# Attention events of the last three passes of a unit, placed without the clamp

## The chip, the cores and the metric

One NeuronCore of a Trainium2 chip runs the kernel. The metric is device time in microseconds (us): the median of three runs. Five engines work side by side, each through its own instructions in order: PE (TensorE, matrix products, with PEld for its weight loads), DVE (VectorE), ACT (ScalarE), POOL (GpSimd) and SP (SyncE, which here issues transfers only). PE writes its results to eight PSUM banks, from which ACT and DVE read them.

## What is computed

```python
def _attn_ref(q, k, v):                       # 8 batches, 12 heads, 448 tokens, 64 wide
    scale = 1.0 / np.sqrt(q.shape[-1])
    scores = scale * np.matmul(q, k.transpose(0, 1, 3, 2))
    attn = np.maximum(scores, 0.0) ** 2 / S
    return np.matmul(attn, v)
...
x = attn_out.transpose(0, 2, 1, 3).reshape(B * S, H * D)   # 3584 x 768
gate = np.maximum(x @ w_gate, 0.0)            # 768 x 1536
val = x @ w_val
out = gate * val @ w_out                      # 1536 x 768
```

Attention with squared ReLU in place of softmax, and behind it a gated feed-forward layer over all 3584 tokens. Inputs and output are float32; the products run in bf16.

## The kernel before

The kernel overlaps two kinds of work on PE: the attention of one batch, and the gate and value products of the batch before.

**Gate/value units.** `gv_units(b)` gives twelve units for batch b, each for 128 of the 1536 hidden columns. A unit (`gv_unit`, L302) is a list of twelve steps, here called passes 0 to 11; a pass is four matmuls of 64x64 weights by 448 tokens (`mm4`, recorded on L72, `ps<-x,gv`). All twelve passes add into one pair of banks, 6 and 7 or 4 and 5 in turn (`acc`). In the last pass ACT writes the ReLU of the gate half to `g_sb` (L320) and DVE multiplies it with the value half into `hT` (L321). Then the pair is free for the unit after next.

**Attention events.** A batch has 21 score tiles and 3 values events.
- A score tile (`scores_event`, L657) is four matmuls (`ps<-kqT`) into a pair of banks; ACT writes the ReLU of both banks to `r_sb` (L232) and DVE squares that into `attn` (L233).
- A values event (`values_event`, L660) is 28 matmuls (`ps<-attn,vn`) into a pair of banks; ACT reads the first bank (L266) and DVE the second (L267), and DVE copies halves across partitions (L261). For the last two batches both engines read parts of both banks (L276, L277).
- All of them take turns on two pairs, banks 0 and 1 and banks 2 and 3 (`sc_later`). So an event can start once the pair of the event before last has been read.

In this text 7.12 is score tile 12 of batch 7, and "values 5.1" is the second values event of batch 5. A place 6:8 is unit 6 of the list, ahead of pass 8.

**Where events go.** The main loop (L745) runs over b = 1 to 6. In each turn the units of batch b - 1 are the frame (ten of them at b = 1, since two were begun before; twelve otherwise). For b = 1 to 4 the events of batch b are spread over them, and for b = 5 and 6 a stream of all that is left of batches 5, 6 and 7. `stream` lists the events in order, and `paced` (L724) gives each a place: it lays out the passes from `first` to `behind` in a row, computes a gap in passes per event (3.8 to 4.4 at b = 1, 2, 5 and 6, and 6.2 at b = 3 and 4, with shorter gaps around values events), and sets each event ahead of the pass at which it falls due. The place is then clamped: where the due pass is 9, 10 or 11 of its unit, the event goes ahead of pass 8 (`len(units[u]) - 4`). Some other events are placed by hand and not by `paced`: the third values event of batches 1 to 4 and of 7 (`last`, 8 or 5), the transposes, the regroup copies with DMA transposes (`turned`), weight sums and loads. `spread` (L686) sorts all events by place and issues them between the passes; every instruction is pinned to the program's order on its engine.

The six turns are six stretches of the run: b = 1 from 36 to 65 us, b = 2 to 102 us, then the output products of the first two batches (`out_pair`), b = 3 from 126 to 161 us, b = 4 to 196 us, output products again, b = 5 from 220 to 261 us, b = 6 to 302 us. After that come output products and the gate/value products of the last two batches (`gv_pair`), with no attention in them.

Of the kernel before, what the change touches and what calls it, by code (L numbers as in the profile page):

```python
# [16 lines left out]
def kernel(  # L17
# [552 lines left out]
    def gv_units(b):  # L570
        b0 = b - b % 2
        if b == b0:
            hT_of[b0] = hpool.tile([128, KF, 2 * S], BF16, name="hT")
        return [gv_unit(b, mf, BEGUN, rotation((BEGUN_IN[mf],))) if b == 0 and mf < 2 else
                gv_unit(b, mf, BEGUN if mf == 0 else STRAIGHT, acc) for mf in range(KF)]
# [148 lines left out]
    def paced(units, first, behind, events):  # L724

        at = [(u, n) for u in range(len(units)) for n in range(len(units[u]))][first:behind]
        gaps = [{(1, 1): 1, (1, NC): 0.35, (NC, 1): 0.75}[a[3], b[3]] for a, b in zip(events, events[1:])]
        gap = len(at) / (sum(gaps) + 1)
        places, due = [], gap / 2
        for (*_, e, _), g in zip(events, gaps + [0]):  # L730
            u, n = at[int(due)]
            places.append((u, min(n, len(units[u]) - 4), e))
            due += g * gap
        return places

# [4 lines left out]
    units = gv_units(0)  # L740
# [4 lines left out]
    for b in range(1, B - 1):  # L745
        if b != B - 2:
            new_x(b)
        units = units[2:] if b == 1 else gv_units(b - 1)
        last = len(units) - 1
        if b < B - 3:  # L750
            first, behind = {1: (28, 109), 2: (40, 132)}.get(b, (0, 132))
            events = paced(units, first, behind, stream(b, b + 1))
            events.append((last, 8 if b == 1 else 5, values_event(b, NQ - 1)))
        else:
            todo = [e for e in attention if e[:2] <= ENDS[b]]
            del attention[:len(todo)]
            events = paced(units, 0, 144 if b == B - 3 else 132, todo)
            if b == B - 2:
                events.append((last, 5, values_event(B - 1, NQ - 1)))
# [75 lines left out]
```

## Time and profile before

| | |
|---|---|
| runs of the kernel, median of 3 | 405.57 us (405.12 to 405.96) |
| the profiled execution | 405.62 us |
| its span, first to last instruction | 403.8 us |
| granted PE clock, mean of the span | 0.999 |
| score tiles' ReLU on ACT (L232) | 167, 0.932 us each |
| gate ReLU on ACT (L320) | 72, 0.548 us each |
| gate times value on DVE (L321) | 72, 0.620 us each |
| squares on DVE (L233) | 167, 0.623 us each |

The span is what the trace covers; 1.8 us of the execution lie around it. A group's line gives its count, the busy time and the mean in ns of one, and behind the bar the time for which the engine stood idle just ahead of these instructions, with what ended that. A line of the order of time gives start, length and a number of like instructions that were merged; a bracket gives idle time ahead of it. All 7376 matmuls of the program have a record in this trace, so that each can be matched with its place in the program.

### The profile page before, as it was taken

How to read it: one execution, taken by the hardware profiler on the slowest of the kernel's cores; microseconds unless marked ns; L12 is line 12 of the kernel's file. 1: busy time of each engine (PE TensorE's matmuls, PEld its weight loads, DVE VectorE, ACT ScalarE, POOL GpSimd, SP SyncE). 2: the span in 40 equal slices, each digit the busy share in tenths (PEclk: the TensorE clock that was granted, in tenths of full speed). 3: DMA queues.
4: the chain of work that ended last, by engine and by line, in shares of the span. 5: the costliest groups of instructions: out<-in, count | busy, mean ns of one | idle time of the engine just before them, and what ended most of it. 6: DMA issues, size and time to landing. Idle time of an engine off the chain costs nothing.

```text
span 403.8 us, 16572 instructions
## 1 busy us (share of the span) xinstructions
PE 392.3 (97%) x7376; PEld 275.9 (68%) x7376; DVE 304.4 (75%) x532; ACT 243.8 (60%) x358; POOL 95.6 (24%) x164
## 2 busy tenths in 40 slices
PE   7799999999999999999999999999999999999995
PEld 4466767778776666666677677687777766777664
DVE  5975896599944686787833988988889969997751
ACT  3961984797334776877423889899973233444221
POOL 8933300710223601205344020020003230000230
PEclk9999999999999999999999999999999999999999
DMA  9999998999836894957946559562001350000144
GB/s 153 170 195 197 197 178 98 160 205 175 129 89 174 107 164 79 139 111 93 191 95 174 93 85 136 92 92 29 3 2 38 91 151 3 2 3 3 42 124 112
DMA packets 90983, 44.16 MB, mean 109 GB/s; under 512 B 55424, under 2 KB 89952, under 8 KB 90912
## 3 DMA queue, kind: packets, MB, share of 16 engines
q0 software_dynamic: 51136, 28.58, 49.6%
q1 hardware_dynamic: 39104, 13.99, 18.5%
q8 instruction: 57, 0.93, 1.0%
q10 hardware_dynamic: 672, 0.54, 0.5%
q14 instruction: 14, 0.11, 0.1%
HBM read 47.19 MB, written 11.01 MB: 144 GB/s over the span
## 4 chain that ended last, share of the span: by engine, by line
PE 86%; DVE 6%; ACT 5%; DMA 1%; issue 1%; DVEq 0%; ACTq 0%
PE ps L72 85%; ACT r_sb L232 4%; DVE attn L233 2%; DMA kr<-in_k_dram 1%; ACT g_sb L320 1%; PE ps L208 1%; DVE kqT L209 1%; DVE x L261 0%; PE ps L217 0%; DVE attn L399 0%; DVE hT L321 0%; DVE kn L277 0%; DVE r_sb L615 0%; DVE x L638 0%; DVE vn L349 0%
## 5 line engine op out<-in xcount | busy, mean ns | idle before, releaser
L72 PE MATMUL ps<-x,gv 64*64 64x448 bf16 x3552 | 203.4, 349 | 0.5 <-ACT r_sb L232 0.3
L72 PEld LDWEIGHTS <-gv 64*64 64x64 bf16 x4032 | 139.1, 107 | 54.5 <-issue 2.6
L232 ACT ACTIVATE r_sb<-ps 128x896 bf16<-128x896 f32 x167 | 147.6, 932 | 18.6 <-PE ps L72 15.7
L233 DVE TENSOR_TENSOR attn<-r_sb 128x896 bf16<-128x896 bf16 x167 | 102.4, 623 | 30.9 <-ACT r_sb L232 26.8
L72 PE MATMUL ps<-kqT 64*64 64x448 bf16 x672 | 68.4, 352 | 4.4 <-ACT r_sb L232 3.3
L72 PEld LDWEIGHTS <-hT 128*64 128x64 bf16 x1056 | 56.2, 110 | 20.8 <-issue 1.7
L409 POOL DMA_DIRECT2D out_dram<-attn x60 | 31.5, 530 | 153.0 <-DVE attn L399 120.2
L395 ACT ACTIVATE attn<-ps 128x384 f32<-128x384 f32 x64 | 28.8, 450 | 64.0 <-PE ps L72 63.9
L72 PE MATMUL ps<-wo,hT 128*64 128x384 bf16 (+1 forms) x720 | 53.9, 306 | 0.0
L321 DVE TENSOR_TENSOR hT<-ps,g_sb 128x448 bf16<-128x448 f32 x72 | 44.5, 620 | 8.9 <-ACT g_sb L320 8.2
L320 ACT ACTIVATE g_sb<-ps 128x448 bf16<-128x448 f32 x72 | 39.3, 548 | 18.6 <-PE ps L72 18.3
L399 DVE TENSOR_TENSOR attn<-ps,attn 128x384 f32<-128x384 f32 (+1 forms) x48 | 22.8, 504 | 33.4 <-ACT attn L395 19.4
L72 PEld LDWEIGHTS <-kqT 64*64 64x64 bf16 x672 | 27.5, 106 | 19.6 <-issue 9.6
L72 PEld LDWEIGHTS <-vn 64*64 64x64 bf16 (+1 forms) x840 | 30.9, 107 | 12.9 <-issue 2.3
L72 PE MATMUL ps<-attn,vn 64*64 64x448 bf16 x672 | 37.0, 350 | 0.1
L513 ACT ACTIVATE kqT<-ps 128x896 f32<-128x896 f32 x18 | 16.5, 918 | 25.0 <-PE ps L72 25.0
L116 POOL DMA_DIRECT2D vn<-in_v_dram x36 | 23.6, 672 | 19.6 <-DMA wo<-in_moe_w_out_dram 10.1
L675 POOL COPY flag<-kqT 128x1 bf16<-128x1 bf16 x12 | 2.8, 236 | 106.8 <-DMA kqT<-kr 59.9
L72 PE MATMUL ps<-o_ring,hT 128*64 128x384 bf16 (+1 forms) x336 | 25.8, 306 | 0.1
L517 DVE TENSOR_TENSOR kqT<-ps,kqT 128x896 f32<-128x896 f32 x18 | 19.5, 1086 | 5.8 <-PE ps L72 4.2
L266 ACT ACTIVATE x<-ps 128x448 bf16<-128x448 f32 x15 | 8.2, 543 | 14.3 <-PE ps L72 14.3
L261 DVE COPY x<-x 64x896 bf16<-64x896 bf16 x36 | 15.2, 421 | 2.0
(104 smaller groups left out, 287.2 us busy)
## 6 DMA issues: line engine op xcount, KB each, us to landing
out_dram<-attn SPq DMA_DIRECT2D x48, 96.0 KB, 2.5
out_dram<-attn POOLq DMA_DIRECT2D x46, 96.0 KB, 2.4
kn<-in_k_dram POOLq DMA_DIRECT2D x7, 384.0 KB, 6.5
qn<-in_q_dram POOLq DMA_DIRECT2D x7, 384.0 KB, 8.3
vn<-in_v_dram POOLq DMA_DIRECT2D x14, 192.0 KB, 9.1
gv<-in_moe_w_gate_dram POOLq DMA_DIRECT2D x6, 384.0 KB, 11.6
gv<-in_moe_w_val_dram POOLq DMA_DIRECT2D x6, 384.0 KB, 12.0
wo<-in_moe_w_out_dram POOLq DMA_DIRECT2D x2, 1152.0 KB, 13.4
```

Of the source, the lines that this page charges most:

```text
L72: pin(nc.tensor.matmul(o, lhsT=l, rhs=r, start=start, stop=stop, skip_group_check=True))
L116: pin(nc.gpsimd.dma_start(out=o, in_=i))
L232: pin(nc.scalar.activation(r, src, AF.Relu))
L233: pin(nc.vector.tensor_tensor(dst, r, r, ALU.mult))
L261: pin(nc.vector.tensor_copy(x1[p], x0[other]))
L320: pin(nc.scalar.activation(g_sb, o[0], AF.Relu, scale=float(out_scale)))
L321: pin(nc.vector.tensor_tensor(hT[:, mf, col:col + S], o[1], g_sb, ALU.mult))
L395: pin(nc.scalar.activation(out_of(t, r, c), bank(P, t), AF.Copy))
L399: pin(nc.vector.tensor_tensor(o, bank(Q, t), o, ALU.add))
L409: pin(engines[c].dma_start(out=rows[:, c0:c1, :], in_=src))
L513: pin(nc.scalar.activation(held(n, j), both(PQ[n][0]), AF.Copy))
L517: pin(nc.vector.tensor_tensor(k, both(PQ[n][1]), k, ALU.add))
```

## The change

```diff
@@ def paced(units, first, behind, events) @@
         for (*_, e, _), g in zip(events, gaps + [0]):
             u, n = at[int(due)]
-            places.append((u, min(n, len(units[u]) - 4), e))
+            places.append((u, n, e))
             due += g * gap
         return places
```

An event that falls due at pass 9, 10 or 11 of its unit now goes ahead of that pass, and no longer ahead of pass 8. Events that fall due at pass 0 to 8 keep their place, as do those placed by hand; `evenly` (L696), which has the same clamp, is not called. Worked out from the code, 38 of the 163 events that `paced` places move:

| b | events that move, with unit and due pass (all stood ahead of pass 8) |
|---|---|
| 1 | 1.1 2:9, 1.4 3:9, 1.14 6:11, 1.17 7:11, 1.20 8:11 |
| 2 | 2.1 3:10, 2.4 4:11, 2.9 6:9, 2.12 7:10, 2.15 8:11, 2.20 10:9 |
| 3 | 3.1 0:9, 3.3 1:9, 3.5 2:10, 3.7 3:10, 3.9 4:11 |
| 4 | 4.1 0:9, 4.3 1:9, 4.5 2:10, 4.7 3:10, 4.9 4:11 |
| 5 | 5.2 0:11, 5.7 2:9, 5.10 3:11, 5.15 5:9, values 5.1 5:10, 5.18 6:11, 6.2 8:9, 6.5 9:11, 6.10 11:9 |
| 6 | 6.13 0:10, 6.16 1:11, 7.3 4:9, 7.6 5:10, 7.9 6:11, 7.12 7:11, 7.17 9:9, 7.20 10:9 |

The set of instructions is the same. On PE each moved event's matmuls stand one to three passes later. On ACT, POOL and SP the order of instructions is unchanged. On DVE one regroup copy (L180, of `kn` into `kr` at b = 2) comes ahead of the square of 2.20 and no longer behind it.

## The prediction

> **What bounds the kernel.** I read the page's busy shares first, then busy time by stretch for the six stretches in which events are spread over gate/value units, then the order of time on PE and ACT where PE's starts spread apart.
>
> ```profile
> PE 392.3 (97%) x7376; PEld 275.9 (68%) x7376; DVE 304.4 (75%) x532; ACT 243.8 (60%) x358; POOL 95.6 (24%) x164
> PEclk9999999999999999999999999999999999999999
> ```
>
> ```profile
> 36.00:65.00 29.00, 28.41 (x589) 20.20 (x585) 23.30 (x43) 22.41 (x31) 5.43 (x9) 1.00 1.40 180
> 65.00:102.00 37.00, 37.00 (x772) 28.76 (x765) 28.41 (x50) 26.16 (x38) 10.09 (x15) 1.00 1.14 163
> 126.00:161.00 35.00, 35.00 (x744) 21.65 (x744) 24.83 (x46) 25.65 (x35) 7.62 (x16) 1.00 0.80 124
> 161.00:196.00 35.00, 35.00 (x748) 21.65 (x743) 26.23 (x47) 26.19 (x36) 10.04 (x16) 1.00 0.87 121
> 220.00:261.00 41.00, 40.28 (x839) 28.36 (x838) 35.18 (x65) 35.46 (x49) 5.27 (x9) 1.00 0.69 107
> 261.00:302.00 41.00, 40.53 (x836) 31.00 (x826) 35.41 (x63) 36.72 (x54) 3.38 (x6) 1.00 0.24 36
> ```
>
> Columns: stretch, length, busy PE, PEld, DVE, ACT, POOL, clock. PE is the bound and its clock is full. But ACT is at 86% and 90% of stretches 5 and 6, against 73% in stretches 3 and 4. "Busy" hides PE's short waits, since matmuls overlap; the starts show them:
>
> ```profile
> 286.52 0.46 PE L72 MATMUL ps<-kqT 64*64 64x448 bf16 x4
> 286.71 0.46 PE L72 MATMUL ps<-x,gv 64*64 64x448 bf16 x4
> 287.63 0.38 PE L72 MATMUL ps<-kqT 64*64 64x448 bf16 x4 [0.45 <-ACT r_sb L232]
> 287.82 1.71 PE L72 MATMUL ps<-x,gv 64*64 64x448 bf16 x32
> 289.33 0.39 PE L72 MATMUL ps<-kqT 64*64 64x448 bf16 x4
> ```
>
> A pass costs (289.33 - 287.82)/8 = 0.189 us, a score tile the same (287.63 to 287.82). From 286.71 to 287.63 one pass took 0.92: PE stood for 0.73 us before score tile 7.12, whose bank pair (that of 7.10) ACT had not yet read. What ACT did then:
>
> ```profile
> 286.65 2.54 ACT L232 ACTIVATE r_sb<-ps 128x896 bf16<-128x896 f32 x3
> 289.04 0.59 ACT L320 ACTIVATE g_sb<-ps 128x448 bf16<-128x448 f32 x1
> 289.76 1.86 ACT L232 ACTIVATE r_sb<-ps 128x896 bf16<-128x896 f32 x2
> 291.52 0.54 ACT L320 ACTIVATE g_sb<-ps 128x448 bf16<-128x448 f32 x1
> ```
>
> 7.10's relu started at 286.65 and ended at 287.58, so 7.12 started 0.05 after it. Relus queued on ACT follow each other by (2.54 - 0.92)/2 = 0.81; a free ACT starts a relu 0.43 after the tile's matmuls (289.33, 289.76).
>
> I took this excess over 0.189 at every pass. In us: stretch 1: 0.08 before values 1.0, 0.41 before tile 1.14, 0.20 inside 1.17, 0.27 before 1.20. Stretch 2: 0.05 before 2.4, 0.19 before values 2.0, 0.11 before unit 8, 0.20 before 2.15. Stretches 3 and 4: none; every event's bank was free 0.75 or more before its start. Stretch 5: 0.44 before values 5.1, 0.12 before values 5.2, 0.83 inside 6.10. Stretch 6: 0.17 before values 6.1, 0.14 before 7.0, 0.11 before values 6.2, 0.21 inside 7.3, 0.19 before values 7.0, 0.73 before 7.12, 0.08 before values 7.1, 0.08 inside 7.17. Each wait but unit 8's is for a score bank; about 4.6 us in all, and the most that better placing can win.
>
> **The change, part by part.** Nothing is added or removed. Of the events, 37 score tiles and one values event (5.1) issue 1 to 3 passes later on PE. ACT, POOL and SP keep their order, so no DMA is moved past another; on DVE one 0.55 us regroup copy changes places with one square. Costs:
>
> ```profile
> L232 ACT ACTIVATE r_sb<-ps 128x896 bf16<-128x896 f32 x167 | 147.6, 932 | 18.6 <-PE ps L72 15.7 <-ACT g_sb L320 1.5
> L320 ACT ACTIVATE g_sb<-ps 128x448 bf16<-128x448 f32 x72 | 39.3, 548 | 18.6 <-PE ps L72 18.3
> L321 DVE TENSOR_TENSOR hT<-ps,g_sb 128x448 bf16<-128x448 f32 x72 | 44.5, 620 | 8.9 <-ACT g_sb L320 8.2
> ```
>
> An event that waits gains what the passes now ahead of it cover: 0.19, 0.38 or 0.57. What it costs is a later relu, where ACT was not already behind; that delay lasts until ACT next stands idle, or meets the next event that waits. So I walk along, event by event, with a relu at the later of its tile's start + 0.43 and the ACT instruction before it.
>
> *Stretch 1.* 1.1 and 1.4, one pass later each, push ACT by 0.13, of which 0.08 reaches values 1.0 (at 47.55, no slack): -0.08. 1.14 moves by 0.57 over a wait of 0.41: +0.41. Values 1.1 gives back 0.15, because 1.14's relu ends no sooner (55.46 before, 55.55 then). 1.17, in pass 11, then arrives at 58.43, just when DVE ends reading values 1.1's bank (58.38, later by 0.08): the 0.15 returns, with 0.02 more. 1.20 needs 1.18's relu, which ends at 61.38 either way; PE would be there at 61.33, so 0.10 of its wait stays: +0.17. Together 0.52, which nothing takes back: values 1.2 has slack 1.56, and the next units are limited by PE alone.
>
> *Stretch 2.* 2.4: +0.06. 2.15: +0.20, given back at 2.17, whose second bank waits for DVE's copy of values 2.1 (ends at 94.26 either way; that chain starts at 2.13's relu and a 1.36 us weight sum). The waits at values 2.0 and unit 8 stay. Net 0.06.
>
> *Stretches 3 and 4.* Ten moves, 0. What covers them: slack of 0.75 to 2. Nearest is 3.9 (and 4.9), from pass 8 to 11 of unit 4: the gate relu comes 0.5 later, and unit 6, which needs the bank, had 0.83 (0.79) of slack. Without that cover each would cost up to 0.5.
>
> *Stretch 5.* Values 5.1 two passes later: +0.35 of its 0.44. Then 5.18, three passes later, lets ACT stand for 0.33 that it had worked through, and values 5.2 waits 0.41 in place of 0.12: 0.06 is left. 6.5 shifts DVE's full chain (regroups, squares, values 6.0) by 0.07; 6.10, one pass later, gains 0.19 less that.
>
> *Stretch 6.* Values 6.1 takes this back, so PE is then 0.07 late, as ACT is. 7.3: +0.19, taken back at values 7.0. 7.12: 0.57 later against a wait of 0.73: PE is 0.50 earlier than before (0.57 less the 0.07). ACT's idle 0.13 and 0.12 at 7.13 and 7.14 go, so values 7.1 comes 0.26 earlier, and 7.17's pass covers 0.10 more: 0.36. The output products behind it run on PE without a gap in the chain of waits (287.6 to 389.7), so it reaches the end.
>
> Sum: 0.52 + 0.06 + 0 + 0 + 0.36 = 0.94 off the span of 403.8, or off 405.62 for the profiled execution. That stands 0.05 above the median, so I forecast 405.57 - 0.94 = 404.63, called 404.7 since a wait can reappear where I took slack of 0.05 as enough. Bounds of the unknown (how much of a gain survives the next wait): all, or none with ACT's delays passed on; they are the last two rivals.
>
> **Rivals.**
> *ACT decides the late stretches* (chance 0.18): what 7.12 wins is taken back at values 7.1, and only stretches 1 and 2 count: 405.57 - 0.58 = 405.0. For it: ACT at 90%, and my own walk loses five gains this way. Against it: ACT stands idle at 7.13 and 7.14.
> The Trainium skill ("Perfetto Trace Analysis", section Identifying the Most-Contended Engine) holds matmul occupancy to be a poor measure and wants TensorE judged by weight-load time instead. In stretch 6 that is 31.00 of 41, 76%, under ACT's 90%, so by this rule ACT is the engine to relieve there and this rival is the outcome.
>
> *All gains stay* (0.12): 0.43 (1.14 with its refill) + 0.22 + 0.27 + 0.07 + 0.22 (2.15) + 0.44 + 0.19 + 0.03 (6.13) + 0.19 + 0.57 + 0.10 = 2.7: 402.9. Against it: the values events follow closely and wait already.
>
> *Slower, by relus ahead of the gate's relu* (0.12). Fourteen tiles now stand before pass 11, where their 0.93 relu precedes the unit's L320, then L321, which frees the accumulator for the unit after next. It decides where the slack there is under 0.57. The rows give 0.8 to 2.4, save 0.28 (unit 11 of stretch 5) and none (unit 3 of stretch 6): 0.29 + 0.57 = 0.86. If ACT's delays at 5.2, 5.7, 5.10 and 6.5 (0.31 + 0.20 + 0.35 + 0.22 = 1.08) are passed on too, and my 0.94 is won: 405.57 + 0.86 + 1.08 - 0.94 = 406.6. Against it: at nine of the fourteen ACT is behind already, and the gate's relu moves by 0.13 or less.
> The Trainium skill ("TensorE: Matmul & The Clock Gate", Part 1, architectural detail) says that ScalarE's and VectorE's queues are strictly first in, first out, so no gate relu can pass a score relu.
>
> *It does nothing here* (0.06): waits merely move on: 405.57.
>
> **How the numbers follow.** Forecast case 0.52, from 404.2 to 405.1. A measurement of this kernel can tell about 0.2% (0.81 us) from no change; the line is 404.76. Of the forecast case 0.31 lies below it; with 0.12 and 0.03 of the first rival: faster 0.46. Same: 0.21 + 0.15 + 0.06 + 0.02 = 0.44. Slower: 0.10. The range leaves out most of the all-stay case and the far half of the slow one: 403.9 to 405.9.
>
> **What would show it.** Right: 7.12, 1.14 and values 5.1 start less than 0.2 after the pass before them; values 5.2 waits longer; stretches 3 and 4 keep their length to 0.1. Wrong: units that start late behind L321; stretch 1 shortened by less than 0.3, or stretch 6 lengthened.

## The result, and the profile after

| | before | after |
|---|---|---|
| median of 22 runs each | 405.49 us | 403.86 us |
| ratio, with its 95% interval | | 0.9966 (0.9953 to 0.9979) |
| span of the profiled execution | 403.8 us | 401.9 us |

The changed kernel is faster by 0.34%, which is 1.4 us (0.9 to 1.9); the medians alone stand 1.6 apart. The ratios here leave out two runs far off the rest: one of 1049.05 us of the kernel before, and one of 510.95 us of "only batches 5 to 7" below. The forecast was 404.7 with a range of 403.9 to 405.9: the median lies 0.04 below that range, while the ratio on the 405.57 from which the forecast started gives 404.2 (403.7 to 404.7). The engines' busy times on the page hardly move, and the clock is full, as before:

```profile
PE 390.4 (97%) x7376; PEld 280.8 (70%) x7376; DVE 303.4 (75%) x532; ACT 243.2 (60%) x358; POOL 96.0 (24%) x164
PEclk9999999999999999999999999999999999999999
```

PE's busy time falls from 392.3 to 390.4, although it runs the same matmuls. That is not the gain: 1.2 of it lies ahead of tile 1.2 (36.24 to 35.01), where of the change only the move of 1.1 lies. Behind it busy time falls by 0.64 (356.05 to 355.41) and idle time by 0.78 (6.28 to 5.50), so of the waits that went the record had counted some as busy and some as idle. Next, busy time by stretch, the windows moved to where the six stretches now lie (columns as before):

```profile
35.50:64.00 28.50, 28.48 (x602) 22.06 (x600) 23.59 (x43) 22.33 (x31) 5.54 (x8) 1.00 1.38 183
64.00:101.00 37.00, 37.00 (x771) 32.68 (x764) 28.54 (x50) 26.41 (x38) 10.10 (x15) 1.00 1.15 165
125.00:160.00 35.00, 35.00 (x748) 21.65 (x744) 24.69 (x45) 25.67 (x35) 7.80 (x16) 1.00 0.81 126
160.00:195.00 35.00, 35.00 (x748) 21.60 (x740) 25.95 (x46) 26.22 (x36) 10.51 (x16) 1.00 0.88 121
219.00:259.50 40.50, 40.01 (x836) 27.35 (x834) 34.81 (x65) 34.77 (x48) 5.12 (x9) 1.00 0.72 108
259.50:300.50 41.00, 40.92 (x841) 32.08 (x832) 36.07 (x64) 36.82 (x55) 3.25 (x6) 1.00 0.24 36
```

ACT does the same work in the same order, so its shares stay at 86% and 90% in the last two. What moved is seen in the order of time on PE, at tile 7.12:

```profile
285.12 0.46 PE L72 MATMUL ps<-kqT 64*64 64x448 bf16 x4
285.31 1.03 PE L72 MATMUL ps<-x,gv 64*64 64x448 bf16 x16
286.23 0.38 PE L72 MATMUL ps<-kqT 64*64 64x448 bf16 x4
286.42 1.14 PE L72 MATMUL ps<-x,gv 64*64 64x448 bf16 x20
287.36 0.39 PE L72 MATMUL ps<-kqT 64*64 64x448 bf16 x4
```

and on ACT beside it:

```profile
285.25 2.54 ACT L232 ACTIVATE r_sb<-ps 128x896 bf16<-128x896 f32 x3
287.64 0.59 ACT L320 ACTIVATE g_sb<-ps 128x448 bf16<-128x448 f32 x1
288.06 1.79 ACT L232 ACTIVATE r_sb<-ps 128x896 bf16<-128x896 f32 x2
289.66 0.63 ACT L320 ACTIVATE g_sb<-ps 128x448 bf16<-128x448 f32 x1
```

Four passes (x16) now stand between 7.11 and 7.12, where one stood. They take 0.92 us (285.31 to 286.23), 0.76 of it work: the wait is 0.16 and no longer 0.73. 7.12 starts as long after 7.10's relu as before (0.98 us, 285.25 to 286.23; it was 286.65 to 287.63), for that is what it waits for. But three passes that came after it are now done ahead of it. And behind 7.12 ACT catches up: from the gate's relu to the next, 289.66 - 287.64 = 2.02 us, where it took 2.48 (289.04 to 291.52), because 7.13 and 7.14 are there when ACT is.

The groups on ACT and DVE cost the same to 0.6% (L232 took 932 ns each, and now 937); the idle time ahead of them shifts:

```profile
L232 ACT ACTIVATE r_sb<-ps 128x896 bf16<-128x896 f32 x167 | 148.5, 937 | 19.4 <-PE ps L72 17.6 <-ACT g_sb L320 0.4 <-DVE attn L233 0.2
L321 DVE TENSOR_TENSOR hT<-ps,g_sb 128x448 bf16<-128x448 f32 x72 | 44.6, 620 | 9.1 <-ACT g_sb L320 8.5
L320 ACT ACTIVATE g_sb<-ps 128x448 bf16<-128x448 f32 x72 | 39.4, 549 | 18.2 <-PE ps L72 17.9
```

**Length by stretch.** Since all matmuls have their records, each event's start can be compared between two executions. This table, worked out from those starts, gives by how much each kernel's trace differs from the trace of before, in us; its rows are the kernels of the experiments below, one trace each. "Ahead" is the start of tile 1.2, which only tile 1.1 of all that moves precedes on PE; stretch 1 counts from there to its last pass. The output products between the stretches are left out: they keep their length to 0.05, save -0.15 with the clamp at pass 5 and +0.17 with 6.10 later.

```
                     ahead  str.1  str.2  str.3  str.4  str.5  str.6
the change           -0.48  -0.66  +0.02  +0.00  -0.00  -0.36  -0.38
only batches 1, 2    -0.45  -0.41  +0.09  +0.00  +0.00  +0.00  +0.00
only batches 5 to 7  +0.28  +0.00  +0.12  +0.00  +0.00  -0.36  -0.38
twelve moves         +0.09  -0.76  +0.31  +0.00  +0.00  -0.57  -0.47
the other 26         +1.44  +0.11  +0.18  -0.00  +0.00  +0.20  +0.14
twelve, less 1.17    -0.94  -0.33  +0.12  +0.00  +0.00  -0.57  -0.48
values later         -0.72  -0.76  +0.86  +0.00  +0.00  -0.11  -0.47
6.10 later           -0.31  -0.67  +0.24  +1.27  +0.00  -0.74  -0.17
combined             -0.14  -0.76  +0.45  +0.00  +0.00  -0.98  -0.06
combined, sums       -0.98  -0.78  +0.30  +0.00  +0.00  -0.99  -0.06
clamp at pass 5      -0.35  +1.93  +2.41  +0.00  +0.00  +3.27  +2.89
```

In the change the stretches give 1.38 us, which is what the runs' ratio gives (1.4). The 0.48 ahead is not the change's: it goes from -0.98 to +1.44 in other kernels, among them "only batches 5 to 7" (+0.28), whose instructions there are those of the kernel before. That kernel is a control for stretch 1 too (0.00), and "only batches 1, 2" for stretches 5 and 6 (0.00). Stretch 2 is less steady: kernels whose events move alike there differ by up to 0.22 (the change +0.02, "only batches 1, 2" +0.09, "6.10 later" +0.24), so smaller differences in that column say nothing of an edit by themselves.

### The profile page after: what moved, and what is told of

It is laid out like the page before. It is cut to its first block, busy times and chain, and to the rows that moved or that the text cites. A ratio compares the mean times of both kernels' runs of the same rounds, so it can differ in the third digit from the quotient of the medians.

```text
span 401.9 us, 16572 instructions
## 1 busy us (share of the span) xinstructions
PE 390.4 (97%) x7376; PEld 280.8 (70%) x7376; DVE 303.4 (75%) x532; ACT 243.2 (60%) x358; POOL 96.0 (24%) x164
## 4 chain that ended last, share of the span: by engine, by line
PE 89%; DVE 4%; ACT 2%; DMA 1%; issue 1%; POOL 1%; POOLq 0%; DVEq 0%; ACTq 0%
PE ps L72 88%; DVE attn L233 2%; ACT r_sb L232 2%; DMA qn<-in_q_dram 1%; PE ps L208 1%; DVE kqT L209 1%; POOL qn L116 0%; DVE attn L399 0%; POOL kn L116 0%; DVE kn L277 0%; DVE x L638 0%; DVE vn L349 0%; DVE hT L321 0%; DVE qr L180 0%; ACT g_sb L320 0%
## 5 line engine op out<-in xcount | busy, mean ns | idle before, releaser
L72 PEld LDWEIGHTS <-gv 64*64 64x64 bf16 x4032 | 143.4, 107 | 50.6 <-issue 2.6
L232 ACT ACTIVATE r_sb<-ps 128x896 bf16<-128x896 f32 x167 | 148.5, 937 | 19.4 <-PE ps L72 17.6
L321 DVE TENSOR_TENSOR hT<-ps,g_sb 128x448 bf16<-128x448 f32 x72 | 44.6, 620 | 9.1 <-ACT g_sb L320 8.5
```

The costliest lines, as they stand in the source:

```text
L72: pin(nc.tensor.matmul(o, lhsT=l, rhs=r, start=start, stop=stop, skip_group_check=True))
L232: pin(nc.scalar.activation(r, src, AF.Relu))
L321: pin(nc.vector.tensor_tensor(hT[:, mf, col:col + S], o[1], g_sb, ALU.mult))
```

## The experiments

All change `paced` alone, save one that also moves the weight sums. Some choose which events keep the clamp, some move events on from where the change put them, and the last sets the clamp three passes further the other way. Each edit stands against the changed kernel unless the text says otherwise, and shows the lines that matter. In the edits `late` is a set of (batch, number), and `b, t` come from the event, with `w` for its kind (`NC` for a values event).

**Which stretch.**

```diff
-            places.append((u, n, e))
+            places.append((u, n if b <= 2 else min(n, len(units[u]) - 4), e))    # and b >= 5
```

> Only the events of batches 1 and 2 lose the clamp (11 moves). Waits filled where they stand (my theory): stretch 1 ends 0.67 us earlier against tile 1.2, as in the changed kernel, stretch 2 adds nothing (0.0 to -0.05), stretches 3 to 6 keep their length to 0.1; about 404.8 us in all, ratio 0.998. Rival, the late stretches bring nothing because ACT decides there: this kernel is as fast as the whole change, ratio 0.9966.

> Only the events of batches 5 to 7 lose the clamp (17 moves). My theory: stretches 5 and 6 together 0.75 us shorter, as in the changed kernel (0.37 and 0.38), the others unchanged; about 404.7 us, ratio 0.998. Rival, ACT decides the late stretches: within 0.1 us of the kernel before.

Ratios 0.9980 (0.9959 to 1.0001) and 0.9985 (0.9968 to 1.0002), each too near 1 to tell by itself. The traces tell: the one gains 0.32 in stretches 1 and 2 and nothing elsewhere, the other 0.74 in stretches 5 and 6 and nothing elsewhere but for stretch 2, which reads +0.12 there though none of its events moved. The rival that ACT's share leaves nothing to gain in the late stretches falls: over half of the gain is there.

Stretch 1 gained 0.41 there and not the 0.66 that the same instructions gave in the changed kernel. DVE's order of time in "only batches 1, 2" shows why:

```profile
58.96 0.63 DVE L233 TENSOR_TENSOR attn<-r_sb 128x896 bf16<-128x896 bf16 x1
59.95 0.56 DVE L180 COPY qr<-qn 128x1536 bf16<-128x1536 bf16 x1 [0.36 <-DMA qn<-in_q_dram]
60.43 0.62 DVE L233 TENSOR_TENSOR attn<-r_sb 128x896 bf16<-128x896 bf16 x1
60.96 0.62 DVE L321 TENSOR_TENSOR hT<-ps,g_sb 128x448 bf16<-128x448 f32 x1
```

A regroup copy stood for a load of q (0.36 us, last column), and with it the product of unit 7 (L321), which ended at 61.58. Unit 9 needs that bank pair, and PE stood 0.24 inside its first pass. In the changed kernel the copy did not wait, and 0.09 us were left between that product and unit 9, where before there were 0.86. So the accumulators' slack, the place of the slower rival, does decide here once something else is late.

**Which events.**

```diff
+        late = {(1, 14), (1, 17), (1, 20), (2, 4), (2, 15), (5, 15), (5, 16), (6, 10), (6, 13), (7, 3), (7, 12), (7, 17)}
-            places.append((u, n, e))
+            places.append((u, n if (b, t) in late else min(n, len(units[u]) - 4), e))    # and: not in late
```

> Only the twelve events that PE waited for, or that stand right ahead of one (1.14, 1.17, 1.20, 2.4, 2.15, 5.15, values 5.1, 6.10, 6.13, 7.3, 7.12, 7.17), lose the clamp. My theory: all gains of the change without the delays that the other moves pass to ACT: stretch 1 0.77 us shorter, stretches 5 and 6 0.8 us, so 0.2 us better than the whole change; values 5.2 waits 0.12 us as before and not 0.22. Rival, even spacing as such gives the gain: well under the whole change, about 12/38 of its gain (0.4 us). Rival, slower by relus ahead of the gate's: units behind 1.17, 1.20 and 7.12 start late behind L321.

> The other 26 moves alone. My theory: no wait is filled and ACT's relus come later, so stretch 1 is 0.1 us longer, stretches 3 and 4 unchanged, stretches 5 and 6 together 0.1 to 0.4 us longer; ratio 1.000 to 1.001. Rival, even spacing as such gives the gain: 0.9 us faster than before (26/38 of the gain).

The twelve alone: ratio 0.9962 (0.9947 to 0.9977), by the runs not to be told from the whole change. By the trace stretches 1, 5 and 6 are 1.80 us shorter, against 1.40. The other 26: ratio 1.0011 (0.9994 to 1.0029), and 0.45 longer in the same stretches. So the gain is not that of even spacing: it comes from the events that PE waited for, and the other moves take a quarter of it back. Half of that, 0.21, they take in stretch 5, on ACT. In the changed kernel, ACT's order of time ahead of values 5.2:

```profile
241.62 0.92 ACT L232 ACTIVATE r_sb<-ps 128x896 bf16<-128x896 f32 x1 [0.23 <-PE ps L72]
242.44 0.54 ACT L320 ACTIVATE g_sb<-ps 128x448 bf16<-128x448 f32 x1
242.86 1.74 ACT L232 ACTIVATE r_sb<-ps 128x896 bf16<-128x896 f32 x2
244.46 0.58 ACT L320 ACTIVATE g_sb<-ps 128x448 bf16<-128x448 f32 x1
244.88 1.78 ACT L232 ACTIVATE r_sb<-ps 128x896 bf16<-128x896 f32 x2
```

and in the kernel with the twelve:

```profile
240.36 2.72 ACT L232 ACTIVATE r_sb<-ps 128x896 bf16<-128x896 f32 x3
242.96 0.55 ACT L320 ACTIVATE g_sb<-ps 128x448 bf16<-128x448 f32 x1
243.44 1.80 ACT L232 ACTIVATE r_sb<-ps 128x896 bf16<-128x896 f32 x2
245.18 0.54 ACT L320 ACTIVATE g_sb<-ps 128x448 bf16<-128x448 f32 x1
```

as it was in the kernel before:

```profile
241.02 2.72 ACT L232 ACTIVATE r_sb<-ps 128x896 bf16<-128x896 f32 x3
243.62 0.55 ACT L320 ACTIVATE g_sb<-ps 128x448 bf16<-128x448 f32 x1
244.10 1.80 ACT L232 ACTIVATE r_sb<-ps 128x896 bf16<-128x896 f32 x2
245.92 0.54 ACT L320 ACTIVATE g_sb<-ps 128x448 bf16<-128x448 f32 x1
246.36 1.72 ACT L232 ACTIVATE r_sb<-ps 128x896 bf16<-128x896 f32 x2
```

With 5.18 moved to pass 11 ACT stands 0.23 us ahead of its relu (the bracket); with 5.18 at pass 8 three relus, those of 5.16, 5.17 and 5.18, follow one another in one row, with hardly a gap. Values 5.2 then waits 0.22 in the first, and stretch 5 ends 0.21 later than in the second (-0.36 against -0.57).

In stretch 2 the twelve came out 0.31 longer, which was not expected. There one of DVE's weight sums waits for the output weights to land (0.2 us in this trace, none before), the copy of values 2.1 behind it is late, and 2.17 waits 0.44 for it. The next kernel moves the same events in stretch 2; there the sum did not wait, 2.17 waited 0.16, and the stretch came out only 0.12 longer. So most of the 0.31 goes with when the weights landed in this execution.

**Does a gain live alone?** Against the kernel with the twelve:

```diff
-        late = {(1, 14), (1, 17), (1, 20), ...
+        late = {(1, 14), (1, 20), ...
```

> The eleven events of the twelve that PE waited for, without 1.17, which stays ahead of pass 8. My theory (a gain lives only until the next event whose bank frees at a fixed time): what 1.14 wins (0.41) is handed back at 1.17, whose second bank DVE frees no earlier, so stretch 1 is only 0.2 to 0.35 us shorter than before, and not 0.76 as with 1.17; stretches 5 and 6 as with the twelve (0.57 and 0.47 shorter). Rival, each move wins its own wait by itself: stretch 1 0.56 us shorter (0.76 less 0.20).

It ran once (403.37 us), so its trace alone counts. Stretch 1 is 0.33 shorter, against 0.76 with 1.17: taking out one move whose own wait was 0.20 costs 0.43. PE's order of time there:

```profile
56.40 0.39 PE L72 MATMUL ps<-kqT 64*64 64x448 bf16 x4
56.59 0.39 PE L72 MATMUL ps<-x,gv 64*64 64x448 bf16 x4
56.78 0.38 PE L72 MATMUL ps<-kqT 64*64 64x448 bf16 x2
57.44 0.38 PE L72 MATMUL ps<-kqT 64*64 64x448 bf16 x2 [0.28 <-DVE x L267]
```

1.17 begins at 56.78 and its second pair of matmuls stands until 57.44, when DVE has read the second bank of values 1.1. There PE stands for what 1.14 had won.

**The waits that are left.** Most of them stand before values events. The gaps around these are changed so that each spread values event comes one or two passes later, and its neighbours stay:

```diff
-        gaps = [{(1, 1): 1, (1, NC): 0.35, (NC, 1): 0.75}[a[3], b[3]] for a, b in zip(events, events[1:])]
+        gaps = [{(1, 1): 1, (1, NC): 0.6, (NC, 1): 0.5}[a[3], b[3]] for a, b in zip(events, events[1:])]
```

> The changed kernel, and besides each spread values event one or two passes later, with its neighbours where they were. The waits left in the changed kernel stand mostly before values events (0.18, 0.16, 0.26, 0.05, 0.22, 0.11, 0.33, 0.11, 0.33, 0.27 us). My theory: each is filled by up to 0.19 us, 1.5 us if nothing took it back, and some of it is handed back at the second tile behind each values event: 0.6 to 1.2 us faster than the changed kernel, 1.9 to 2.6 us faster than before, ratio 0.994 to 0.9955. Rival, ACT decides: 0 to 0.2 us faster than the changed kernel.

This missed: ratio 0.9973 (0.9955 to 0.9991), not better than the change. Against the change, stretches 1 and 6 gained 0.1 each, but stretch 2 lost 0.84. On DVE, first in the changed kernel, then in this one:

```profile
83.08 0.62 DVE L267 CAST x<-ps 128x448 bf16<-128x448 f32 x1 [0.17 <-PE ps L72]
83.81 0.79 DVE L261 COPY x<-x 64x896 bf16<-64x896 bf16 x2
84.63 1.36 DVE L345 TENSOR_TENSOR qn<-wo 128x2304 bf16<-128x2304 bf16 x1
```

```profile
83.11 1.36 DVE L345 TENSOR_TENSOR qn<-wo 128x2304 bf16<-128x2304 bf16 x1 [0.61 <-DMA wo<-in_moe_w_out_dram]
84.38 0.62 DVE L267 CAST x<-ps 128x448 bf16<-128x448 f32 x1
85.10 0.79 DVE L261 COPY x<-x 64x896 bf16<-64x896 bf16 x2
```

Values 2.0 had moved from pass 6 to 7 of its unit, and the weight sum stands at pass 6 by hand: so the sum came ahead of the copy out of values 2.0's bank. The bank was free 1.29 us later than in the changed kernel, although PE came to values 2.0 0.40 earlier, and PE stood 0.95 for it at 2.10. Stretch 5 gained 0.25 less than in the changed kernel: DVE stood 3.2 us for output stores ahead of the first square, where in the changed kernel it did not, the square ended 1.9 us later against PE, and unit 2 and tile 5.10 then waited 0.09 and 0.23 for DVE. How much of that is the edit was not tried.

The wait inside 6.10 (0.66 left) is for DVE's read of values 6.0:

```diff
+            places.append((u, 11 if (b, t, w) == (6, 10, 1) else n, e))
```

> The changed kernel with tile 6.10 two passes later, ahead of pass 11. Its wait of 0.66 us is for DVE, which reads values 6.0 late behind four regroup copies. My theory: the wait falls by 0.38, and stretch 5 is 0.35 us shorter than in the changed kernel; of that, values 6.1 takes back most, since ACT's relus of 6.11 to 6.14 do not move: stretch 6 0.2 to 0.35 us longer. Rival, the wait moves to another place of stretch 5: nothing gained there.

Stretch 5 is 0.38 shorter than in the changed kernel and stretch 6 is 0.21 longer, as expected: ACT keeps what comes behind. Its one run, 405.39 us, is slower than the change. What its trace shows for that lies in stretch 3, whose events stand as in the changed kernel. DVE there:

```profile
130.14 1.16 DVE L233 TENSOR_TENSOR attn<-r_sb 128x896 bf16<-128x896 bf16 x2 [4.53 <-DMA out_dram<-attn]
131.22 0.62 DVE L321 TENSOR_TENSOR hT<-ps,g_sb 128x448 bf16<-128x448 f32 x1
```

The first squares of stretch 3 write a buffer that the output stores are still reading; DVE stood 4.53 us for them (1.8 before, 2.7 in the changed kernel), the product of unit 0 queued behind the squares, and PE stood for it:

```profile
131.89 0.94 PE L72 MATMUL ps<-x,gv 64*64 64x448 bf16 x14 [1.08 <-DVE hT L321]
```

**Together.** The twelve, 6.10 ahead of pass 11, values events later (with the `late` and `gaps` of above); then the same with the weight sums one pass later as well, behind values 2.0 again:

```diff
+            n = 11 if (b, t, w) == (6, 10, 1) else n if w == NC or (b, t) in late else min(n, len(units[u]) - 4)
+            places.append(max((u, n), places[-1][:2] if places else (0, 0)) + (e,))
...
-            events += [(last - 5 + 2 * n, 6, lambda n=n: weight_sums(2 * n)) for n in range(2)]
+            events += [(last - 5 + 2 * n, 7, lambda n=n: weight_sums(2 * n)) for n in range(2)]
```

> The twelve moves that pay, tile 6.10 ahead of pass 11, and the values events one or two passes later. My theory: the sum of the parts less what is handed back, 0.7 to 1.4 us faster than the changed kernel, ratio 0.993 to 0.995 against before. Rival, ACT decides: no better than the twelve alone (0.9962).

> As the twelve moves with later values events and later 6.10, and the two weight sums one pass later, so that DVE reads values 2.0 ahead of the 1.36 us sum again. My theory: the wait at 2.10 (0.95 us where the sum stood ahead of the copy) goes, stretch 2 is at most 0.15 us longer than before instead of 0.45, the other stretches as without this: about 0.3 us better, ratio 0.994 to 0.995. Rival, the landing of the output weights sets stretch 2: no change, +0.4 to +0.5.

Ratios 0.9951 (0.9932 to 0.9969) and 0.9943 (0.9923 to 0.9963). The wait at 2.10 is gone in the second, as expected, but stretch 2 is still 0.30 longer than before and not 0.15: the other weight sum, moved too, now stands between the squares of 2.14 and 2.15, DVE's copy of values 2.1 comes behind it, and 2.17 waits 0.54 for that copy. In stretches 5 and 6 they gain 1.04 and 1.05 in all, as the twelve did by themselves (1.04): 0.4 more in stretch 5, 0.4 less in stretch 6. So the 0.7 to 1.4 us over the change that I expected of the first did not come: summed over the stretches it gains 1.35 and the second 1.53, against 1.38 of the change and 1.49 of the twelve. The last one has the best ratio of all, ahead of the change by 0.2%, which the intervals don't separate.

**The clamp three passes further the other way, at pass 5.**

```diff
-            places.append((u, n, e))
+            places.append((u, min(n, len(units[u]) - 7), e))
```

> The suspected cost doubled: the clamp is at pass 5, so events due at passes 6 to 11 all go ahead of pass 5 (72 events or more). My theory: each event that has to wait for its bank loses the passes that stood ahead of it, up to 0.57 us more at each of the places where the kernel before waits for ACT (1.14, 1.20, 2.4, 2.15, 7.12) and new waits in stretches 3 and 4: 2 to 6 us slower than the kernel before. Rival, the accumulators' slack decides (gate relu earlier is better): no slower, or faster, since every gate relu is then free of score relus.

415.43 us, ratio 1.0241 (1.0212 to 1.0270): 10 us slower, above the 2 to 6 expected. In PE's waits, of the change and of this kernel (engine, line, whom it waited for, us, times, longest):

```profile
PE ps L72 <- ACT r_sb L232: 3.0, 7, 0.6
```

```profile
PE ps L72 <- ACT r_sb L232: 7.9, 21, 0.6
```

Against no clamp that is 11.9 us by the starts (10.5 and the 1.4 of the change), over eight times what the clamp at pass 8 costs; the idle time that these lines put down to ACT shows 4.9 of it. The new waits are not where I expected them: stretches 3 and 4, whose events lie 6.2 passes apart, lose nothing at all, and all 10.5 us fall on the stretches with a gap of about 4 passes. Gate relus free of score relus won nothing in those two stretches (0.00), and outweighed nothing in the others.

## Why the prediction was right, point by point

- *The sign and the mechanism* held. 1.14, values 5.1 and 7.12 now wait 0.00, 0.05 and 0.16, where they waited 0.41, 0.44 and 0.73; values 5.2 waits longer; stretches 3 and 4 kept their length to 0.00. The time came from the waits for score banks: the twelve moves at or right ahead of a wait gave 1.80 in stretches 1, 5 and 6, and the other 26 lost 0.45 there.
- *The size* was too small: 0.94 forecast, 1.38 by the trace. Stretch 1 gave 0.66 for 0.52, stretch 2 -0.02 for 0.06, stretches 5 and 6 together 0.74 for 0.36. That the two late stretches are over half of the gain is not what the prediction's sum says (0.36 of 0.94).
- *The term that was mis-sized most* is "values 5.2 waits 0.41 in place of 0.12: 0.06 is left". It waits 0.22, and 0.31 is left. I let ACT's delay behind 5.18 run on unchanged. But ACT stood only 0.23 idle and then caught up: from the start of 5.18's relu to that of 6.0's it took 3.26 us (241.62 to 244.88), where it had taken 3.53 (242.83 to 246.36), since what came behind 5.18, the next gate's sums above all, was there when ACT was.
  The same reckoning failed once more at "Values 6.1 takes this back, so PE is then 0.07 late": PE came to values 6.1 with 0.36 in hand (values 6.0 had taken 0.11, 6.10 added 0.17), values 6.1 took 0.16 of it, and PE went on 0.20 early. These 0.27 are most of what stretches 5 and 6 gave beyond the forecast.
- *Stretch 1*: "1.18's relu ... ends at 61.38 either way" was wrong. ACT had stood 0.15 idle ahead of it; it came earlier with PE, and 1.20 waits 0.00, not 0.10. Also, 0.07 that PE had stood ahead of pass 2 of unit 6, which the prediction's list leaves out and for which the trace names no one waited for, went as well. The 0.08 put down to 1.1 and 1.4 was 0.10, and the 26 moves show it alone: stretch 1 0.11 longer.
- *Stretch 6* ran as walked from 7.3 on, though from 0.20 early and not 0.07 late: 7.3 hands back at values 7.0; 7.12 waits 0.16; behind it PE keeps 0.37 past values 7.1; 7.17 adds 0.10.
- *The rival that ACT decides* is out by "only batches 5 to 7". *All gains stay* is out by the 1.38, against 2.7, and by 1.17, without which the 0.41 of 1.14 is lost whole. *Slower by relus ahead of the gate's* has the right place but the wrong price: slack at the units behind moved tiles fell by up to 0.77 (unit 9 of stretch 1), and by 0.57 as worked out at two units of stretch 6, but it was used up only where a transfer was late too, and at unit 3 of stretch 6, which had none before either (-0.08, then -0.16, for a wait of 0.04).

## What to carry to other kernels

Find waits by the spacing of starts, not by busy or idle time: of the 0.73 us ahead of 7.12 the record showed 0.45 as idle, and the rest stood inside "busy". Where an engine waits for a buffer, put work that does not need the buffer ahead of the wait, and only there; the 26 moves at places that did not wait only delayed the engines behind, by 0.45 in all. A gain lives until the next wait whose end it does not move, so follow it to the end of the stretch, and look at what is issued by hand at the same place (the weight sum) before moving anything past it.

## What the runs showed that I had not expected

Two differences between executions are as large as the effect. The start-up ahead of tile 1.2 spread over 2.4 us (-0.98 to +1.44) in twelve traces, that of before among them, whose instructions up to 1.1 are the same. And the first squares of stretch 3 stood between 1.6 and 4.53 us for output stores where they stood for them at all. In stretches 1, 5 and 6, comparing starts event by event separated effects of 0.1 us that the runs' intervals, some 0.3% to 0.4% wide, could not; in stretch 2, where a transfer's landing takes part, it did not go below 0.2.
